# q's second half ahead of the weights, column 0 by feature tile, and a new list for the opening

## The chip, the cores and the metric

The program runs on one core of a Trainium2 chip. The metric is the device time in microseconds of one execution, taken as the median of several. The engines are TensorE (PE, with its weight loads as PEld), VectorE (DVE), ScalarE (ACT), GpSimd (POOL) and SyncE (SP), which here only issues DMAs.

## What is computed

Three layers, one after the other, in float32. Attention with 32 packed rows per head, twice (first the packed rows against k and v, then q against the packed rows), a gated layer, and a layer with a leaky ramp:

```python
def sm_attn(qq, kk, vv):            # scale, max, exp, sum, divide, times vv
    ...
p_packed = sm_attn(p, k, v)         # batch 8, heads 8, seq 576, head_dim 64, 32 packed rows
x = sm_attn(q, p_packed, p_packed)  # -> 4608 tokens x 512
gate = 1.0 / (1.0 + np.exp(-(x @ w_gate)))   # 512 x 1536
x = gate * (x @ w_val) @ w_out               # 1536 x 512
h = x @ w_in                                 # 512 x 2048
out = np.maximum(0.01 * h, h) @ w_out        # 2048 x 512
```

The weights arrive as 64-bit numbers and are read as pairs of 32-bit words.

## The kernel before

**Precision.** TensorE multiplies in a short float32 form, so an operand is split in a high part (a cast on ACT) and a low part (a subtraction, mostly on DVE), and three products stand for one: low by high, high by low, high by high.

**Weights.** A weight tile is loaded as 1024 word pairs per partition (L363). `unit` turns it into float32 in five passes: ACT scales the upper words (L307), ACT converts the lower words (L316), ACT puts in the sign (L324), DVE shifts (L332), POOL adds (L338). `unit_gv(i, g)` does this for column block i (256 features, two feature tiles of 128) of the gate weights (g = 0) or the value weights (g = 1); 6 column blocks, `wc[i]`. Column 0 alone is loaded and converted in two parts, by rows of the weights.

**Attention.** `attention(b)` loads k (L485), p (L479), q in two halves (L494) and v (L503, L507) of batch b; transposes k (L525, L529), p (L510) and q (L521) on DVE; scores of the packed rows (L540), their maximum (L568), exp (L576), sums and reciprocals (L587, L588), scaling (L594), flips through TensorE (L602) and copies (L612, L613), product with v (L622), packing (L634 to L650). Then q's scores (L540 again) in two halves of the tokens: `front` transposes them in PSUM (L655), takes the maximum (L663), subtracts it (L665) and takes exp (L674); `back` sums (L681, L682, L686), scales (L687), transposes (L695) and splits the weights of attention into `Ah` (L708, ACT) and `Al` (L710, DVE).

**Gated layer.** `gated(b)` multiplies the packed rows with column block i first (`m_mm`, L815, 16 matmuls), splits the result (`m_split`: cast to `mh`, L829, subtraction to `ml`, L832), and multiplies it with `Ah` and `Al` for each of 12 feature tiles f: 12 matmuls for the gate, 12 for the value (L848). ACT takes tanh (L857), DVE combines (L863), SP stores the tile to `g1d` in DRAM (L870).

**Other weights.** Beside the gated layers of all batches `staged` prepares 22 tiles of the three other weight matrices on ACT, DVE and POOL and stores them to DRAM (wp, wu and wd in the rows).

**Blocks.** Then five blocks of tokens (480 or 384 twice) go through the last three products, with 4620 matmuls (L1030), in Strassen's scheme of 7 products. Their weights come back from DRAM through SP (`load_weights`, L942, 512 KB each, tile name wu), their inputs from `g1d` through POOL's DMA queue (L1110), and are split by ACT (L971) and DVE (L976).

**Order.** No engine chooses by itself at run time: each does its instructions in the order in which they were written. `Plan` writes that order. Each task has an engine, a duration, a rank (lower goes first), tasks that it follows, and places in pools that it takes and gives. The plan runs through its own time; on each engine the ready task of lowest rank is written next. Urgent tasks that are soon ready keep others from starting. Between plan times 2 and 100 an idle PE gets filler matmuls (`keep`, L1271). The staged tiles have ranks from 200 in steps of 22; `open_left`, after which the first weight loads of the blocks may be written, follows when all staged tiles have begun their stores.

Of the kernel before, what the change touches and what calls it, by code (L numbers as in the profile page):

```python
# [10 lines left out]
F32 = mybir.dt.float32  # L11
# [8 lines left out]
P = 128  # L20
# [11 lines left out]
class Plan:  # L32
# [9 lines left out]
    def __init__(self):  # L42
        self.tasks, self.pools, self.holders, self.table = [], {}, {}, None
        self.begun, self.slots, self.where, self.lag = {}, {}, {}, {}
        self.urgent, self.keep = set(), None
# [5 lines left out]
    def add(self, engine, us, rank, fn, after=(), take=(), give=(), table=None, slack=None, begun=(), lag=3.5, urgent=False):  # L51
        i = len(self.tasks)
        if urgent:
            self.urgent.add(i)
        self.lag[i] = lag if engine == "DMA" else 0
# [10 lines left out]
    def run(self):  # L66
# [16 lines left out]
        soon = {e: {} for e in ready}  # L83
        while len(order) < n:
            for e, heap in ready.items():
# [3 lines left out]
                while heap:  # L89
# [7 lines left out]
                    if all(  # L97
# [82 lines left out]
def pack_attention_glu_lrelu(  # L180
# [100 lines left out]

    def unit(key, rank, dma_rank, loads, target, apart, home="raw64", after=()):

# [13 lines left out]
        def rows4(x, h):  # L297
            k = x.shape[1] // m
            return x[:, k * h:k * h + k]

        def scale(h):
            def fn():
                if "x" not in t:
# [3 lines left out]
                nc.scalar.activation(  # L307
                    x, word.rearrange("p (a b) -> p a b", a=x.shape[1]), AF.Copy, scale=2.0 ** -112
                )
# [34 lines left out]
        for h in range(len(loads)):  # L344
            L.append(add("DMA", 3.4 / len(loads), dma_rank + 0.1 * h, do_load(h),
# [3 lines left out]
        for h in range(m):  # L349
            need = [L[h]] if apart else L[-1:]  # L350
            a = add("ACT", us[0], rank + 0.1 * h, scale(h), [*need, *after, *made[-1:]])
            c = add("ACT", us[1], rank + 0.1 * h, low(h), [a], take=[("cv", ("cv", key))] if h == 0 else ())
            made.append(add("ACT", us[2], rank + 0.1 * h, sign(h), [c], give=[("raw", key)]))
            s = add("DVE", 0.75 if m == 1 else 0.5, (-91.5 if rank < -90 else -40 if rank < -44 else rank) + 0.1 * h, shift(h), [a])
            ends.append(add("POOL", 2.4 if m == 1 else 1.34, rank + 0.1 * h, total(h), [made[h], s], give=[("cv", key)]))
        return ends

    def unit_gv(i, g):
        w = (w_gate, w_val)[g]

        def load(j0, j1):
# [7 lines left out]
        first = i < 1  # L369
        rank = (-100 if i == 0 else -64 + 16 * i) + 2 * g  # L370
        return unit(
            ("gv", i, g), rank, (-71.05, -70)[g] if i == 0 else -60 + 4 * i + 2 * g, [load(0, 2), load(2, 4)] if first else [load(0, 4)],
            lambda: wc[i][:, :, g], first, HOMES[2 * i + g],
# [5 lines left out]
    def staged(st, g, kk, rank):  # L379
# [54 lines left out]
        a1 = add("POOL", 2.2, rank, combine(  # L434
            (2, 7, 1, ALU.add), (slice(3, 5), slice(2, 7, 4), slice(6, 8), ALU.subtract)
        ), whole)
        a2 = add("POOL", 0.82, rank, combine((5, 0, 3, ALU.subtract)), [a1])
        stored[key] = []
        for a, x0, x1 in ((a1, 0, 4), (a2, 4, 7)):
            n = (x1 - x0) * 256  # L440
            h = add("ACT", act(n), rank - 2000, high(x0, x1), [a], take=[("HL", (key, x0))])
            l = add("POOL", 0.7 + n * 0.0024, rank - 2000, low(x0, x1), [h], give=[y])
# [21 lines left out]
    def attention(b):  # L464
# [234 lines left out]
        def fin(half, part):  # L699
            def fn():  # L700
# [8 lines left out]
                else:  # L709
                    nc.vector.tensor_tensor(  # L710
# [5 lines left out]
        r1 = r0 - (60 if b else 80)  # L716
# [3 lines left out]
        tp = late("DVE", 0.43, r1, p_t, [Lp] + (packed[b - 1, "ck"] if b else []), give=[K("praw")[1]])  # L720
        tk = [
            late("DVE", 0.81 if b < 2 else 0.9, r1 + 0.1 * j, tr("k", j), [Lk[j // 2]], take=[K("w576", "tk", j)],
# [7 lines left out]
        mx = [late("DVE", 0.88 if b < 2 else 0.95, r1 + 2 + G, max1(G), [ck]) for G in range(2)]  # L730
        packed[b, "ck"] = [ck]
        ex = [
            late("ACT", 0.88 if b < 2 else 0.98, r1 + G, exp1(G), [mx[G]], take=[K("w576", "a", G)], give=[K("ps", "sk", G)[1]])
# [4 lines left out]
        r0 -= 20 * (b == 1)  # L738
        fl, un, norms = [], [], []
        for G in range(2):  # L740
# [3 lines left out]
            fl.append(late("PE", 0.8 if b < 2 else 1.25, r0 - 30 + G, flip(G), [nm], take=[K("ps", "f", G)],  # L744
# [559 lines left out]
```

## Time and profile before

| | us |
|---|---|
| three runs | 1426.91, 1429.21, 1429.30 |
| median | 1429.21 |
| profiled execution, its own time | 1425.92 |
| its span in the profile | 1424.1 |
| PE busy | 1408.0 (99%) |
| DVE, ACT, POOL busy | 977.5, 723.3, 474.8 |
| share of the chain that ended last: L1030, L848 | 67%, 22% |

Times in the rows are counted from the start of the span. PE's busy time holds the fillers too, so the opening looks fuller than it is: useful work is PE's time less the time of L1271. The execution has three stages: the opening, to about 71 us, in which batches 0 and 1 start and the fillers run; the gated layers with attention beside them, to 457.43; the blocks, to the end.

### The profile page before, as it was taken

The numbers are of one execution on the slowest core, as the hardware profiler recorded it, in microseconds if no ns is written. First come the engines' busy times: TensorE is split into PE (matmuls) and PEld (weight loads), VectorE is DVE, ScalarE is ACT, GpSimd is POOL, SyncE is SP. The second block draws the span as 40 slices with busy tenths as digits, with TensorE's granted clock in tenths as the row PEclk, the third lists the DMA queues.
The fourth block names the chain that finished last, engine by engine and source line by source line (L and its number), as shares of the span: only waits on it lengthen the run. The fifth ranks groups of instructions, "written<-read, shape, count | busy, mean of one in ns | idle before, by whom it ended". The sixth has DMA issues, their size and how long they took to land.

```text
span 1424.1 us, 24514 instructions
## 1 busy us (share of the span) xinstructions
PE 1408.0 (99%) x9724; PEld 1226.5 (86%) x9724; DVE 977.5 (69%) x1162; ACT 723.3 (51%) x855; POOL 474.8 (33%) x513
## 2 busy tenths in 40 slices
PE   8999999999999999999999999999999999999998
PEld 5788888888888888888888888888888888899997
DVE  6878778778755764778464987546984648785483
ACT  5876766776864434453244634345532446333460
POOL 1426873787885000056000156000460000460002
PEclk9999999999999999999999999999999999999999
DMA  9999998999878876698777798676997766998887
GB/s 316 271 279 312 324 309 272 330 319 336 307 267 322 278 231 205 202 339 256 209 227 203 246 312 242 207 232 198 307 288 208 222 205 210 319 275 253 255 253 184
DMA packets 146354, 374.93 MB, mean 263 GB/s; under 512 B 34544, under 2 KB 45136, under 8 KB 146240
## 3 DMA queue, kind: packets, MB, share of 16 engines
q1 hardware_dynamic: 115248, 295.76, 66.6%
q0 software_dynamic: 25696, 76.96, 15.5%
q8 instruction: 77, 1.26, 0.4%
q10 hardware_dynamic: 5296, 0.64, 0.3%
q14 instruction: 37, 0.30, 0.1%
HBM read 295.17 MB, written 78.12 MB: 262 GB/s over the span
## 4 chain that ended last, share of the span: by engine, by line
PE 95%; DVE 3%; DMA 1%; SPq 0%; issue 0%; ACT 0%; DVEq 0%
PE ps_pair L1030 67%; PE ps_pair L848 22%; PE ps_pair L815 3%; PE ps_pair L540 2%; DMA raw<-in_q_dram 1%; PE ps_pair L622 1%; DVE Al L710 0%; DVE ml L832 0%; DVE wc L332 0%; DMA raw<-in_k_dram 0%; PE ps_pair L1271 0%; PE ps_pair L602 0%; DVE sg L863 0%; DVE mx L663 0%; DVE ps_pair L655 0%; PE ps_pair L643 0%
## 5 line engine op out<-in xcount | busy, mean ns | idle before, releaser
L1030 PE MATMUL ps_pair<-op,wu 128*128 128x480 f32 (+1 forms) x4620 | 959.9, 370 | 0.0
L1030 PEld LDWEIGHTS ps_pair<-op,wu 128*128 128x128 f32 x4620 | 853.4, 188 | 106.3
L971 ACT CAST op<-rg 128x960 fp32r<-128x960 f32 (+1 forms) x280 | 259.6, 963 | 236.6 <-DVE rg L962 133.4
L976 DVE TENSOR_TENSOR op<-rg,op 128x960 fp32r<-128x960 f32 (+1 forms) x280 | 304.1, 1109 | 50.3 <-ACT op L971 49.5
L1110 POOL DMA_DIRECT2D rg<-g1d x96 | 68.7, 718 | 572.0 <-DVE op L976 170.4
L1047 DVE TENSOR_TENSOR tmp<-ps_pair,tmp 128x960 f32<-128x960 f32 (+1 forms) x60 | 67.0, 1117 | 194.3 <-PE ps_pair L1030 140.3
L962 DVE TENSOR_TENSOR rg<-rg 128x960 f32<-128x960 f32 (+1 forms) x160 | 177.4, 1111 | 6.0 <-DMA rg<-g1d 4.7
L848 PE MATMUL ps_pair<-Ah,ml 128*128 128x288 f32 x768 | 172.3, 305 | 0.5 <-DVE ml L832 0.4
L848 PE MATMUL ps_pair<-Al,mh 128*128 128x288 f32 x768 | 164.7, 295 | 0.7 <-DVE Al L710 0.7
L848 PE MATMUL ps_pair<-Ah,mh 128*128 128x288 f32 x768 | 164.8, 295 | 0.0
L848 PEld LDWEIGHTS ps_pair<-Ah,ml 128*128 128x128 f32 x768 | 122.1, 188 | 39.3 <-issue 14.3
L1217 POOL DMA_DIRECT2D out_dram<-os x208 | 124.2, 605 | 76.1 <-DVE os L1197 69.5
L848 PEld LDWEIGHTS ps_pair<-Al,mh 128*128 128x128 f32 x768 | 123.5, 188 | 0.9 <-DVE Al L710 0.9
L848 PEld LDWEIGHTS ps_pair<-Ah,mh 128*128 128x128 f32 x768 | 123.6, 188 | 0.0
L1041 ACT COPY tmp<-ps_pair 128x960 f32<-128x960 f32 (+1 forms) x60 | 55.7, 928 | 119.4 <-PE ps_pair L1030 119.4
L1162 ACT ACTIVATE rg<-rg 128x960 f32<-128x960 f32 (+1 forms) x80 | 78.0, 975 | 73.0 <-DVE rg L1158 71.6
L863 DVE SCALAR_TENSOR_TENSOR sg<-sg,ps_pair 128x576 f32<-128x576 f32 x96 | 71.8, 749 | 57.2 <-PE ps_pair L848 29.1
L417 POOL TENSOR_TENSOR HL<-Y,HL 128x1024 fp32r<-128x1024 f32 (+1 forms) x44 | 95.1, 2172 | 21.5 <-ACT HL L411 21.1
L857 ACT ACTIVATE sg<-ps_pair 128x576 f32<-128x576 f32 x96 | 62.4, 650 | 58.9 <-PE ps_pair L848 56.1
L338 POOL TENSOR_TENSOR Y<-Y,cvf 128x1024 int32<-128x1024 int32 x22 | 52.7, 2396 | 75.7 <-DVE Y L332 32.4
L832 DVE TENSOR_TENSOR ml<-ps_pair,mh 128x1024 fp32r<-128x1024 f32 x48 | 58.2, 1213 | 14.7 <-ACT mh L829 14.6
L829 ACT CAST mh<-ps_pair 128x1024 fp32r<-128x1024 f32 x48 | 48.6, 1012 | 35.9 <-PE ps_pair L815 35.8
(83 smaller groups left out, 938.6 us busy)
## 6 DMA issues: line engine op xcount, KB each, us to landing
wu<-wu SPq DMA_DIRECT2D x140, 512.0 KB, 3.9
wu<-wd SPq DMA_DIRECT2D x140, 512.0 KB, 4.3
wu<-wp SPq DMA_DIRECT2D x105, 512.0 KB, 4.5
g1d<-sg SPq DMA_DIRECT2D x96, 288.0 KB, 4.6
raw<-in_moe_w_out_dram SPq DMA_DIRECT2D x28, 512.0 KB, 6.7
raw<-in_k_dram SPq DMA_DIRECT2D x16, 576.0 KB, 6.4
rg<-g1d POOLq DMA_DIRECT2D x24, 384.0 KB, 6.2
rg<-g1d POOLq DMA_DIRECT2D x18, 480.0 KB, 7.8
```

The lines of the kernel that those rows point to most:

```text
L417: nc.gpsimd.tensor_tensor(out=hl[:, :, 1], in0=t["y"][:, x0:x1], in1=hl[:, :, 0].bitcast(F32), op=ALU.subtract,)
L848: nc.tensor.matmul(ps[:, t, :HS], w, x[:, t * HS:(t + 1) * HS], start=(n == 0), stop=(n == len(pairs) - 1),)
L857: nc.scalar.activation(st["sg", f], st["gv", f, 0][:, :, :HS], AF.Tanh, scale=0.5)
L863: nc.vector.scalar_tensor_tensor(out=sg, in0=sg, scalar=1.0, in1=st["gv", f, 1][:, :, :HS], op0=ALU.add, op1=ALU.mult)
L962: nc.vector.tensor_tensor(out=src(g, o), in0=src(g, a), in1=src(g, b), op=ALU.subtract)
L971: nc.scalar.copy(h, src(g, c))
L976: (nc.gpsimd if on_pool(i, g) else nc.vector).tensor_tensor(out=l, in0=src(g, c), in1=tiles["op", st, i, g][0].bitcast(F32), op=ALU.subtract)
L1030: nc.tensor.matmul(ps[c][:, m, :TB], a, x[:, kk, :], start=(fresh and kk == 0 and y == 0), stop=(end and kk == 1 and y == 2), skip_group_c ...
L1047: nc.vector.tensor_tensor(out=T[x], in0=ps[c][:, :, :TB], in1=T[y], op=ALU.add)
L1110: nc.gpsimd.dma_start(out=t[:, :, t0 - base:t0 - base + m], in_=g1d[b][:, f:f + 2, s0:s0 + m])
L1162: nc.scalar.activation(t, t, AF.Prelu, alpha=0.01, scale=0.5)
L1217: queues[turn % len(queues)].dma_start(out=ob[:, s0:s0 + m, d0:d0 + 32], in_=tiles["os", c][32 * y:32 * y + 32, x, t0:t0 + m],)
```

## The change

Four things are changed; line numbers move by 13 to 43 (L494 becomes L521, L332 L343, L363 L377 or, for column 0, L392, L655 L682, L710 L737, L815 L844, L829 and L832 L865 and L867, L848 L885, L870 L907, L942 L985, L1030 L1073).

1. The second half of q of batch 0 is loaded ahead of all weights. Column 0 is loaded by `unit_first(f)`, one feature tile of 128 features at a time, gate then value. The four loads are as large as before (512 KB) and have pieces of 1 KB in DRAM, not 2 KB.
2. Column 0's packed product and its split for batch 0 go by feature tile: 8 matmuls of 256 columns, a cast and a subtraction of 512, twice.
3. The ranks and durations of the opening's tasks are listed anew, for batches 0 and 1; the third load of column weights stands ahead of batch 1's k, and batch 1's q later. The plan counts that DVE and POOL can't do certain passes at once (`lock`).
4. The staged tiles have ranks from 256.35 in steps of 19.83.

On DVE three of column 0's four shifts stood ahead of the first L655 and the fourth ahead of the second; now two L343 stand ahead of both L682, which stand together, and two behind. The split of the first feature tile (L867) now stands ahead of the first half of `Al` (L737), and batch 1's k transposes (L552), two of which stood ahead of the second half of `Al`, stand behind it.

The options `GS` and `on_pool`, new in the code, are never on.

```diff
+                        if i in self.lock:
+                            begin, end = (now + x for x in self.lock[i])
+                            late = max(0.0, held["POOL" if e == "DVE" else "DVE"] - begin)
+                            us, held[e] = us + late, end + late
...
+    def unit_first(f):
+        def load(g):
+            def fn(raw):
+                nc.sync.dma_start(
+                    out=raw.rearrange("p (g j c) b -> p g j (c b)", g=2, j=NJ)[:, g],
+                    in_=(w_gate, w_val)[g][:, f * 256:(f + 1) * 256].rearrange("(j p) c -> p j c", p=P),
+                )
+            return fn
+
+        return unit(
+            ("gv", 0, f), -100 + 2 * f, (-70.9, -70)[f], [load(0), load(1)],
+            lambda: wc[0].rearrange("p j g (f c) -> p f g j c", f=2)[:, f], True, HOMES[f],
+        )
...
-        ld = (-100, -52.9)[b] if b < 2 else r1
+        ld = (-100, -50.75)[b] if b < 2 else r1
...
-        r0 -= 20 * (b == 1)
+        r0 -= -4.77 * (b == 1)
...
-        Lq = [add("DMA", 2.2 if b < 2 else 2.0, ((-72, -49)[b] if b < 2 else r1 + 3) + G, load_qk(q, "q", G), take=[K("qk", "q", G)], lag=LAG)
+        Lq = [add("DMA", 2.2 if b < 2 else 2.0, ((-72, -37.39)[b] if b < 2 else r1 + 3) + G, load_qk(q, "q", G), take=[K("qk", "q", G)], lag=LAG)
...
+            first = (b, i) == (0, 0)
+            low = {}
+            for f in range(2) if first else (None,):
+                r = -95 + 0.4 * (f or 0) if first else r0 + 16 * i - 60
...
-        rank = 200
+        rank = 256.35
...
-                    rank += 22
+                    rank += 19.83
```

Three places of the new order. First SP's queue at the very start, before:

```order
L494 DMA raw<-in_q_dram 128x576
L494 DMA raw<-in_q_dram 64x576 x2
L503 DMA v<-in_v_dram 64x8x256 x2
L507 DMA v<-in_v_dram 64x8x64
L363 DMA raw_250<-in_moe_w_gate_dram 128x2x512
L494 DMA raw<-in_q_dram 128x576
L494 DMA raw<-in_q_dram 64x576 x2
L363 DMA raw_250<-in_moe_w_gate_dram 128x2x512
L363 DMA raw_333<-in_moe_w_val_dram 128x2x512 x2
```

and after:

```order
L521 DMA raw<-in_q_dram 128x576
L521 DMA raw<-in_q_dram 64x576 x2
L530 DMA v<-in_v_dram 64x8x256 x2
L534 DMA v<-in_v_dram 64x8x64
L521 DMA raw<-in_q_dram 128x576
L521 DMA raw<-in_q_dram 64x576 x2
L392 DMA raw_300<-in_moe_w_gate_dram 128x4x256
L392 DMA raw_300<-in_moe_w_val_dram 128x4x256
L392 DMA raw_338<-in_moe_w_gate_dram 128x4x256
L392 DMA raw_338<-in_moe_w_val_dram 128x4x256
```

The second half of q has moved ahead of the first weight load; the second weight load still follows q and one other weight load.

Second, ACT around batch 1's exp, before (cvf is the lower words of a weight tile, w_804 and w_811 the two halves of batch 1's packed attention):

```order
L576 ACTIVATE w_804,sm<-ps_pair,mx 128x2x9x32
L576 ACTIVATE w_811,sm<-ps_pair,mx 128x2x9x32
L857 ACTIVATE sg<-ps_pair 128x576
L594 ACTIVATE w_804<-w_804,sm 128x576
L594 ACTIVATE w_811<-w_811,sm 128x576
L829 CAST mh<-ps_pair 128x1024
```

and after:

```order
L603 ACTIVATE w_825,sm<-ps_pair,mx 128x2x9x32
L603 ACTIVATE w_839,sm<-ps_pair,mx 128x2x9x32
L865 CAST mh<-ps_pair 128x1024
L335 ACTIVATE cvf<-Y 128x1024
L621 ACTIVATE w_825<-w_825,sm 128x576
L621 ACTIVATE w_839<-w_839,sm 128x576
```

Between the two exps and the two scalings stood one tanh; now a cast and a sign pass stand there.

Third, SP's queue at the end of the gated layers, before (g1d_64 is batch 7's tiles, wp_65 to wp_67 the first weights of the blocks):

```order
L870 DMA g1d_64<-sg 128x576 x8
L942 DMA wu<-wp_65 128x1024
L870 DMA g1d_64<-sg 128x576
L942 DMA wu<-wp_66 128x1024
L870 DMA g1d_64<-sg 128x576
```

and after:

```order
L907 DMA g1d_64<-sg 128x576 x11
L985 DMA wu<-wp_65 128x1024
L985 DMA wu<-wp_66 128x1024
L907 DMA g1d_64<-sg 128x576
L985 DMA wu<-wp_67 128x1024
```

The first weight load of the blocks stood behind 8 of batch 7's 12 stores and stands behind 11.

## Rows read from the trace of the kernel before

**Rows 1.** Windows: stretch, length, then busy time of PE, PEld, DVE, ACT, POOL, PEclk, DMA share, GB/s.

```profile
0.00:42.80 42.80, 35.78 (x453) 26.58 (x453) 29.40 (x62) 26.59 (x38) 8.21 (x11) 0.96 1.02 301
42.80:70.80 28.00, 26.36 (x394) 19.56 (x394) 24.49 (x46) 24.68 (x32) 12.21 (x5) 1.00 0.89 285
70.80:457.40 386.60, 386.08 (x4263) 327.23 (x4264) 282.91 (x448) 265.04 (x346) 261.76 (x191) 1.00 0.90 305
```

**Rows 2.** Windows of the fillers alone (L1271): stretch, length, busy time of PE, PEld.

```profile
0.00:42.80 42.80, 24.64 (x190) 19.02 (x190) 0.96 1.02 301
42.80:70.80 28.00, 4.09 (x29) 2.55 (x28) 1.00 0.89 285
```

**Rows 3.** Chain of waits: start, length, engine, tile, line.

```profile
23.76 1.48 DVE wc L332
...
34.40 1.23 DVE ml L832
...
39.55 0.59 DVE w L525
...
40.98 0.65 DVE Al L710
...
42.85 1.54 PE ps_pair L540 x55
...
444.45 12.98 PE ps_pair L848 x96
```

**Rows 4.** Timeline at 20 us: start, length, engine, line, operation, then idle before and its releaser.

```profile
20.14 0.78 DVE L521 STREAM_TRANSPOSE w<-raw 128x576 f32<-128x576 f32 x1 [6.38 <-DMA raw<-in_q_dram]
...
21.15 0.67 ACT L307 ACTIVATE wc<-raw 128x512 f32<-128x512 f32 x1 [0.91 <-DMA raw<-in_moe_w_gate_dram]
```

**Rows 5.** Timeline from 32 to 39 us: towards the first products of the gated layer.

```profile
32.67 0.75 DVE L710 TENSOR_TENSOR Al<-w,Ah 128x576 fp32r<-128x576 f32 x1
...
33.70 0.65 DVE L332 TENSOR_SCALAR wc<-wc 128x1024 int32<-128x1024 int32 x1
...
35.72 2.40 POOL L338 TENSOR_TENSOR wc<-wc,cvf 128x1024 int32<-128x1024 int32 x1 [6.42 <-ACT cvf L324]
...
36.43 0.38 PE L848 MATMUL ps_pair<-Ah,ml 128*128 128x288 f32 x1
...
36.83 1.90 DVE L687 TENSOR_TENSOR w<-w,sm 128x576 f32<-128x576 f32 x1
```

**Rows 6.** Windows while v comes in, and while column weights come in.

```profile
9.60:13.50 3.90, 3.59 (x47) 2.64 (x29) 3.39 (x10) 2.57 (x6) 0.00 (x0) 1.00 1.13 216
...
19.00:26.00 7.00, 4.52 (x79) 2.54 (x80) 5.69 (x12) 6.00 (x10) 3.17 (x3) 0.76 1.05 381
```

**Rows 7.** Timeline from 49 to 55 us: batch 1's scaling, its flips, ACT's neighbours.

```profile
49.78 0.77 ACT L594 ACTIVATE w<-w,sm 128x576 f32<-128x576 f32 x1 [1.42 <-DVE sm L588]
50.46 0.99 ACT L829 CAST mh<-ps_pair 128x1024 fp32r<-128x1024 f32 x1
...
50.61 0.77 PE L602 MATMUL ps_pair<-ident,w 128*128 128x128 f32 x5 [0.25 <-ACT w L594]
...
53.83 1.37 ACT L324 ACTIVATE cvf<-Y 128x1024 f16<-128x1024 f32 x1
```

**Rows 8.** Timeline of SP's queue: the weight load behind the eleventh store of batch 7.

```profile
456.22 0.43 SPq L942 DMA_DIRECT2D wu<-wp  x1
```

**Rows 9.** DMA issues at 456 to 457 and 444.9 to 457: KB each, median us to landing.

```profile
wu<-wp SPq DMA_DIRECT2D x1, 512.0 KB, 5.9
...
wu<-wp SPq DMA_DIRECT2D x5, 512.0 KB, 7.4
```

**Rows 10.** The page's DMA issues of the whole span, the same loads.

```profile
wu<-wp SPq DMA_DIRECT2D x105, 512.0 KB, 4.5
```

**Rows 11.** Windows around PE's idle time in the opening: the idle stretch, then what follows.

```profile
18.96:21.46 2.50, 0.00 (x0) 0.00 (x0) 1.29 (x4) 1.56 (x3) 0.08 (x1) 1.00 1.06 379
...
22.16:25.57 3.41, 3.41 (x68) 1.62 (x53) 3.35 (x6) 3.35 (x7) 1.95 (x3) 0.50 1.05 384
```

More of the change, by code (lines that the diff above doesn't have):

```diff
@@ L49, in pool, with add @@
         self.slots[name] = list(range(n))
-    def add(self, engine, us, rank, fn, after=(), take=(), give=(), table=None, slack=None, begun=(), lag=3.5, urgent=False):
+    def add(self, engine, us, rank, fn, after=(), take=(), give=(), table=None, slack=None, begun=(), lag=3.5, urgent=False, lock=None):
         i = len(self.tasks)
@@ L83, in run @@
         soon = {e: {} for e in ready}
+        held = {"DVE": 0.0, "POOL": 0.0}
         while len(order) < n:
@@ L344, in unit @@
         for h in range(len(loads)):
-            L.append(add("DMA", 3.4 / len(loads), dma_rank + 0.1 * h, do_load(h),
+            L.append(add("DMA", 3.4 / len(loads) - (0.1 if rank < -90 else 0), dma_rank + 0.1 * h, do_load(h),
                          take=[(home, ("raw", key))] if h == 0 else (), begun=L[:1], lag=LAG))
@@ L441, in staged @@
             h = add("ACT", act(n), rank - 2000, high(x0, x1), [a], take=[("HL", (key, x0))])
-            l = add("POOL", 0.7 + n * 0.0024, rank - 2000, low(x0, x1), [h], give=[y])
+            l = add("POOL", 0.7 + n * 0.0024, rank - 2000, low(x0, x1), [h], give=[y], lock=(0, n * 0.0024))
             stored[key].append(add("DMA", n / 340, rank, store(x0, x1), [l], give=[(key, x0)], lag=6))
@@ L729, in attention @@
         )
-        mx = [late("DVE", 0.88 if b < 2 else 0.95, r1 + 2 + G, max1(G), [ck]) for G in range(2)]
+        mx = [late("DVE", 0.88, r1 + 2 + G, max1(G), [ck]) for G in range(2)]
         packed[b, "ck"] = [ck]
         ex = [
-            late("ACT", 0.88 if b < 2 else 0.98, r1 + G, exp1(G), [mx[G]], take=[K("w576", "a", G)], give=[K("ps", "sk", G)[1]])
+            late("ACT", 0.88, r1 + G, exp1(G), [mx[G]], take=[K("w576", "a", G)], give=[K("ps", "sk", G)[1]])
             for G in range(2)
@@ L754, in attention @@
         p2 = late("PE", 0.45, r0 - 27, pack2, [p1])
-        p3 = late("DVE", 0.3, r0 - 27 if b else -90.8, pack3, [p2], take=[K("pps")], give=[K("ps", "pp")[1]])
+        p3 = late("DVE", 0.3, r0 - 27 if b else -92, pack3, [p2], take=[K("pps")], give=[K("ps", "pp")[1]])
         packed[b] = p3
@@ L762, in attention @@
         sb = []
-        c = late("PE", 1.5, r0 + (-28 if b < 2 else 9), scores2, [p1, *tq], take=[K("ps", "sq", h) for h in range(2)],
+        c = late("PE", 1.5, r0 + (-26.5 if b < 2 else 9), scores2, [p1, *tq], take=[K("ps", "sq", h) for h in range(2)],
                  give=[K("w576", "tq", j)[1] for j in range(NJ)])
@@ L779, in back @@
             a = late("ACT", act(576), r if b else -200, fin(h, 0), [a, begin])
[L780 removed]
+            on_pool = b == 0 and h < 0
+            fins.append(late("POOL" if on_pool else "DVE", 1.6 if on_pool else 0.75, r, fin(h, 1), [a], lock=(0, 1.6 if on_pool else 0.73),
                             give=[K("w576", "u", h)[1]]))
@@ L882, in gated @@
                     g, vv = [
-                        add("PE", 0.8, r - 0.5 + 0.1 * g, mm(f, g, range(1)), [l, ready_a[b][0]], take=[K("ps", f, g)], urgent=True)
+                        add("PE", 0.8, r - 0.5 + 0.1 * g, mm(f, g, range(1)), [low[f % 2 if first else 0], ready_a[b][0]], take=[K("ps", f, g)], urgent=True)
                         for g in range(2)
```

117 lines of the change are left out of this document (67 added, 50 removed).

## The prediction, made before the change was run

> **What bounds the kernel now.** I read the windows by stage first, then the fillers in the same windows, then the chain of waits, then the timeline at the places where the chain leaves PE. The windows show three stages [rows 1]. From 70.8 to 457.4 PE is busy 386.08 of 386.60 us, and the chain runs through PE's matmuls there and in the blocks: what starts earlier at 70.8 ends earlier by as much, and only a hole in PE's row costs anything. Before 70.8 PE's time is mostly fillers, to be taken out [rows 1, 2]: useful work leaves 42.80 - 35.78 + 24.64 = 31.7 us of the first 42.8 us empty, and 28.00 - 26.36 + 4.09 = 5.7 us of the next 28.0. So the opening is where time can be won. There the chain runs over DVE: a shift of column 0's weights at 23.76 (1.48 us, where it needs 0.4), the split `ml` at 34.40, k transposes from 39.55, the second `Al` at 40.98 [rows 3]. The second place to look at is the seam at 457.43 (444.45 + 12.98, [rows 3]), where PE goes from L848 to L1030 with no gap; whatever is late there is a hole of PE.
>
> **Loads of the opening.** Before, q's third transpose waits for its load until 20.14, and the second scaling of column 0 for its own until 21.15 [rows 4]. q's second half goes ahead of one 512 KB load, which at 381 GB/s [rows 6] takes 1.4 us, so the third transpose should start at about 18.5. That alone gives little: the second weight load stands where it stood, behind q and one other weight load, and its scaling stays at about 21.5 to 22. Its shift is in DVE's row ahead of the first L682, behind POOL's first addition, and ends at 23.6. What is gone is the third shift with its wait, so the first L682 starts at about 23.7 and not at 23.76 + 1.48 = 25.24 [rows 3]: 1.5 us.
>
> Pieces of 1 KB in DRAM appear in no weight load of the trace; v's pieces are of 1 KB, and while v comes in the rate is 216 GB/s against 381 for the weights of 2 KB pieces [rows 6]. Bounds: at 381 GB/s a weight load takes 1.4 us and the change costs nothing; at 216 it takes 2.4, two loads are 2.1 us later, 0.3 of it is slack in front of the second shift, and the opening is 1.8 us longer. Below nothing there is no case, as the bytes are the same. I take nothing: the weight rows are the nearer ones, with the same bytes, queue and 128 partitions, where v's loads go to 64 each. The Trainium skill (SBUF — State Buffer, Door 1: The DMA port swizzle) says that a load's rate follows from how many of 16 ports its partitions reach, and that 64 partitions in a row reach 8 of them. By that rule v is slow for its partitions and not for its pieces, and the term is nothing; if pieces of 1 KB were the cause, it is the 1.8 us. The row for v agrees in size but tells the two causes not apart.
>
> **First products.** Before, the first L848 starts at 36.43, after `ml` (34.40 + 1.23 = 35.63, whole) although `Al` was done at 32.67 + 0.75 = 33.42 [rows 3, 5]. Now half a split stands ahead of `Al`, so `Al` ends last: 33.42, less 1.5 for the start above, plus 0.8 because the second L682 no longer fills the wait for the first exp but stands ahead of the maximum (one transpose, 0.79 as L521 takes 0.78, [rows 4]), plus 0.65 for the half split (half of 1.23 and a little), plus 0.6 because L714 meets POOL's fourth addition (before, L687 took 1.90 us while L338 ran from 35.72 for 2.40 us, [rows 5]). That is 34.0, a gain of 2.4.
>
> The second half of `Al` starts the rest. Before, it ends at 40.98 + 0.65 = 41.63 [rows 3], 8.2 us behind the first. Of these 8.2 go: a shift, 0.65 [rows 5]; two k transposes, 40.98 - 39.55 = 1.4 [rows 3]; the block of L687, which by the first half's equal transposes of 0.77 should take about 0.75 and took 1.90, 1.15 [rows 5]; half of the split, 0.6; and 0.5 comes back, since ACT's cast `Ah` is no longer hidden by the k transposes. The second half follows the first by 4.9 and stands at 38.9 to 39.0: **gain 2.6**. As the lost time of this stretch is made up only of such waits, all of it is a shift of the rest.
>
> **Batch 1's flips.** From 39.0, 36 products at 12.98 / 96 = 0.135 us [rows 3] take 4.9, to 43.9; batch 1's scores take 1.5 [rows 3], from 44.2 to 45.7; column 1's packed product ends at 46.7. The next work is batch 1's flips. Before, they started at 50.61, 7.8 after the scores began at 42.8 [rows 1, 7]. Now a cast (0.99) and a sign pass (1.37, [rows 7]) stand between exp and scaling, together 2.4; a tanh (0.65 by its place between the two) leaves it, and the 1.42 us in which L594 waited for DVE [rows 7] are covered: 44.2 + 7.8 + 2.4 - 0.65 - 1.4 = 52.4. PE has only fillers from 46.7 to 52.4, less 0.3 around it: 5.4. Behind it I count 0.85 and 0.9 us ahead of the packed products of columns 2 and 3, which wait for POOL's additions, and 0.25 in small gaps: 7.4 lost against 5.7 [rows 1, 2]: **loss 1.6 to 1.7**. Bounds: if ACT's order costs nothing, 5 of the 7.4 go and the term is a gain of 3; if POOL's additions drag as well, a loss of 3. I take 1.6. The additional 8 short matmuls of the packed product cost 0.1 at most. On SP's queue a third column load now stands ahead of batch 1's k, and its q behind more weights: 1.4 us each [rows 6]. k is wanted only at 40, by DVE's order, and q only by scores behind the products of columns 1 and 2, so I cost both at nothing; that cover gone, they would cost those 1.4.
>
> So the opening gives -2.6 + 1.6 + 0.1 = -0.9, between -3.5 and +2.
>
> **The seam.** This is the part that the words of the change leave out. The last staged tile has rank 256.35 + 21 x 19.83 = 673, not 200 + 21 x 22 = 662; a batch has 100 ranks and takes about 50 us, so the staged work ends some 6 us later, and the plan writes the first weight load of the blocks behind 11 of batch 7's stores, not 8. SP waits at each store for its tile; behind it is queued every load. Before, a weight load stands right behind the eleventh store and was issued at 456.22 [rows 8], 1.2 us ahead of the seam. That one took 5.9 us to land [rows 9], at 462.1: as first load it would have held PE from 457.43 for 4.65 us. So the price is read from the very place: **4.6 us**. Bounds: the median of all such loads, 4.5 us [rows 10], gives 3.3; the five loads of this stretch, 7.4 [rows 9], give 6.2. Nothing hides it: all L848 of batch 7 are done, no product of the blocks has its weights, and the inputs that POOL's queue brings don't depend on this order. The loads behind it come each 1.2 to 1.5 us while a group of 12 products takes 2.5, so there is one hole and not many.
>
> **The clock.** In the opening PE was idle for 2.50 us and the granted clock in the 3.41 us of work after it was 0.50 [rows 11], the lower level; 3.41 x 0.5 = 1.7 us of work lost. The hole at the seam is longer and holds no fillers. Bounds 0 and 1.7; I take the middle, 0.9, since that idle stretch followed only fillers, this one follows dense work.
>
> **The sum.** -0.9 + 4.6 + 0.9 = +4.6. The profiled execution's own time is 1425.92 (1.8 us of it outside the span, which I leave as they are), so a like one of the changed kernel is at 1430.5. The median of the three runs is 3.29 above the profiled execution; I add the sum to the median: **1433.8**.
>
> **Rivals.** First, *no change that can be told* (0.2% of this kernel, 2.9 us, is about what a measurement can tell; the band is 1426.35 to 1432.07). The first load lands in 4.5 us as most do, and the clock stays up: +3.3 - 0.9 = +2.4, 1431.6. It decides at a landing of 5 us. For it: 105 loads have that median [rows 10]; against it: the last transfers of batch 7 and POOL's loads are on the queues at just that time, and the stretch's own loads are the slow ones [rows 9].
>
> Second, *slow weights*: 1 KB pieces go at v's rate, +1.8 on the forecast, 1435.6. For it: the only row of such pieces [rows 6]; against it: that row's partitions differ.
>
> Third, the other side, *faster*: ACT's cast and sign pass are done by the time DVE has batch 1's reciprocals, so the empty 5.4 us before the flips shrink to 1 and one of the two later holes closes: -0.9 - 4.4 - 0.9 = -6.2 for the opening, and with the seam at 3.3 that is -2.9, 1426.3. It decides where the flips start before 48 us. For it: before, L594 waited for DVE and not for ACT [rows 7]; against it: 2.4 us of ACT passes stand in a row that was full, and the gain has to outrun the seam.
>
> Fourth, that the change doesn't do what it says: q's second half early is of no use, since DVE then waits for column 0's second load [rows 4]. I hold this as likely, and it is in the sum: q's share of the gain is small, the third shift's is the 1.5.
>
> **Chances.** Forecast 0.56, slow weights 0.12, no change 0.25, faster 0.07. So slower by over 0.2% 0.68, within 0.2% 0.25, faster 0.07. The range leaves out the faster case and the tails: low 1429.3 (the seam at 3.3, the clock kept and the opening near its lower bound, -3.2), high 1436.8 (the seam at 6.2, the clock at 1.7, the opening at -0.3).
>
> **What would show it.** In the profile after: the third q transpose (L548) at 18.5; first L682 at 23.7; first L885 at 34.0, its second half at 39; fillers alone from 46.7 to 52.4 ahead of L629; the first weight load of the blocks (L985) issued 1 to 2 us ahead of the last L885's end, and PE idle for 4.6 us before the first L1073, with a clock of 0.5 behind it. I am wrong if PE goes from L885 to L1073 without a hole, or if the lost time before 70.8 falls by more than 4 us.

## The result, and the profile after

The changed kernel took 1435.46 us (median of 4; 1434.62 to 1436.63), the kernel before 1428.38 us in the same comparison (1426.91 to 1429.30). The ratio is 1.0055, with an interval of 1.0043 to 1.0068: it is slower by 7.1 us, where 4.6 were forecast. The time lies in the stated range.

From the page of the changed kernel, the busy times and the row of the blocks' products:

```profile
span 1433.2 us, 24570 instructions
PE 1409.9 (98%) x9740; PEld 1228.5 (86%) x9740; DVE 979.9 (68%) x1163; ACT 723.9 (51%) x856; POOL 474.1 (33%) x513
...
L1073 PE MATMUL ps_pair<-op,wu 128*128 128x480 f32 (+1 forms) x4620 | 963.3, 370 | 7.4 <-DMA wu<-wp 7.4
```

The first line to look at is the last one: the blocks' products were 7.4 us idle for their weights. Before, they began without a gap behind L848, whose last products end at 444.45 + 12.98 = 457.43 [rows 3]; the chain of waits before has them as one piece (start, length, what):

```profile
457.43 959.77 PE ps_pair L1030 x4620
```

In the changed kernel a store and a transfer stand in the chain at this place:

```profile
456.36 0.76 DVE sg L900
457.12 0.02 issue
457.13 0.32 SPq L907
457.45 0.05 issue
457.50 12.36 DMA wu<-wp
469.87 0.14 issue
470.00 956.07 PE ps_pair L1073 x4596
```

PE's timeline at the seam shows two waits, and SP's queue what they wait for:

```profile
455.02 0.42 PE L885 MATMUL ps_pair<-Ah,mh 128*128 128x288 f32 x2
462.56 7.20 PE L1073 MATMUL ps_pair<-op,wu 128*128 128x480 f32 x24 [7.12 <-DMA wu<-wp]
470.00 15.23 PE L1073 MATMUL ps_pair<-op,wu 128*128 128x480 f32 x69 [0.24 <-DMA wu<-wp]
```

```profile
454.74 0.80 SPq L985 DMA_DIRECT2D wu<-wp  x2
457.13 0.32 SPq L907 DMA_DIRECT2D g1d<-sg  x1
457.50 12.61 SPq L985 DMA_DIRECT2D wu<-wp  x6
```

PE leaves L885 at 455.4, 2.0 us earlier than before (457.4). The first two weight loads are issued at 454.7 and 455.1, and the first takes 7.7 us to land. The third stands behind the twelfth store, which waits for DVE's last tile; it is issued at 457.5 and takes 12.4 us. Product 25 of the blocks starts at 470.00, 14.6 us behind the end of L885; before it started 5.0 behind it (462.47). So the seam costs 9.5 us. The two spans differ by 9.1: -2.0 in front of the seam, +9.5 at it, +1.4 spread over the blocks, +0.2 in the tail. (The profiled execution of before, 1425.92, was a quick one of its kind, so 9.1 of the spans stand against 7.1 of the medians.)

The granted clock at the seam, by windows of PE's hole and of what follows (stretch, length, busy time of PE, PEld, DVE, ACT, POOL, PEclk, DMA share, GB/s):

```profile
455.44:462.56 7.12, 0.00 (x1) 0.03 (x1) 7.12 (x8) 3.99 (x5) 4.94 (x7) 0.79 1.03 395
462.56:466.06 3.50, 3.50 (x9) 2.94 (x10) 3.46 (x4) 0.00 (x0) 0.00 (x0) 0.50 1.04 410
```

The granted clock is at its lower level (0.50) for the 3.5 us behind the hole, as it was behind the idle stretch of [rows 11].

The opening, from the timeline of all engines:

```profile
18.24 1.44 DVE L548 STREAM_TRANSPOSE w<-raw 128x576 f32<-128x576 f32 x2 [3.96 <-DMA raw<-in_q_dram]
...
19.39 0.66 ACT L320 ACTIVATE wc<-raw 128x512 f32<-128x512 f32 x1 [3.33 <-DMA raw<-in_moe_w_gate_dram]
...
22.06 1.07 DVE L343 TENSOR_SCALAR wc<-wc 128x512 int32<-128x512 int32 x1 [0.55 <-ACT wc L320]
23.05 1.45 DVE L682 STREAM_TRANSPOSE ps_pair<-ps_pair 128x576 f32<-128x576 f32 x2
```

The first product follows at 32.64 (before 36.43, [rows 5]), the second half's first at 38.14, batch 1's flips at 50.97. To see how much of this gain lasts I take PE's timeline and subtract, at a time t, what the useful matmuls started until then take at their usual spacing. What is left is lost time, in us:

| t | 43 | 60 | 72 | 240 | 440 |
|---|---|---|---|---|---|
| before | 33.1 | 36.3 | 40.1 | 46.6 | 52.1 |
| changed | 29.5 | 35.8 | 37.4 | 43.3 | 50.1 |

The opening wins 3.6 us, has given 3.1 back at 60, wins again where the kernel before lost 2.6 us at 64.6, and keeps 2.0 at the end.

### The profile page after: what moved, and what is told of

The parts are those of the page before. It is cut to its first block, busy times and chain, and to the rows that moved or that the text cites. A ratio compares the mean times of both kernels' runs of the same rounds, so it can differ in the third digit from the quotient of the medians.

```text
span 1433.2 us, 24570 instructions
## 1 busy us (share of the span) xinstructions
PE 1409.9 (98%) x9740; PEld 1228.5 (86%) x9740; DVE 979.9 (68%) x1163; ACT 723.9 (51%) x856; POOL 474.1 (33%) x513
## 4 chain that ended last, share of the span: by engine, by line
PE 81%; DMA 1%; DVE 0%; issue 0%; SPq 0%; DVEq 0%
PE ps_pair L1073 67%; PE ps_pair L885 12%; PE ps_pair L844 2%; DMA wu<-wp 1%; PE ps_pair L567 1%; PE ps_pair L649 0%; PE ps_pair L629 0%; PE ps_pair L670 0%; DVE rg L1240 0%; DVE ml L867 0%; DVE tmp L1231 0%; DVE sg L900 0%; SPq L907 0%; DVE op L1019 0%; DVEq L900 0%
## 5 line engine op out<-in xcount | busy, mean ns | idle before, releaser
L1073 PE MATMUL ps_pair<-op,wu 128*128 128x480 f32 (+1 forms) x4620 | 963.3, 370 | 7.4 <-DMA wu<-wp 7.4
L1073 PEld LDWEIGHTS ps_pair<-op,wu 128*128 128x128 f32 x4620 | 855.2, 188 | 115.4 <-issue 7.9
L885 PE MATMUL ps_pair<-Ah,ml 128*128 128x288 f32 x768 | 171.8, 304 | 2.2 <-DVE ml L867 1.9
L885 PE MATMUL ps_pair<-Al,mh 128*128 128x288 f32 x768 | 164.7, 295 | 0.2 <-DVE Al L737 0.2
L885 PE MATMUL ps_pair<-Ah,mh 128*128 128x288 f32 x768 | 164.9, 295 | 0.0
L885 PEld LDWEIGHTS ps_pair<-Ah,ml 128*128 128x128 f32 x768 | 122.3, 188 | 36.6 <-DVE sg L900 10.9
L885 PEld LDWEIGHTS ps_pair<-Al,mh 128*128 128x128 f32 x768 | 123.6, 188 | 0.4 <-DVE Al L737 0.4
L885 PEld LDWEIGHTS ps_pair<-Ah,mh 128*128 128x128 f32 x768 | 123.6, 188 | 0.0
L867 DVE TENSOR_TENSOR ml<-ps_pair,mh 128x1024 fp32r<-128x1024 f32 (+1 forms) x49 | 58.5, 1196 | 17.7 <-ACT mh L865 17.5
L432 POOL TENSOR_TENSOR Y<-Y 128x256 f32<-128x256 f32 (+1 forms) x66 | 63.3, 960 | 4.1
```

The costliest lines, as they stand in the source:

```text
L432: nc.gpsimd.tensor_tensor(out=y[:, o], in0=y[:, a], in1=y[:, b], op=op)
L885: nc.tensor.matmul(ps[:, t, :HS], w, x[:, t * HS:(t + 1) * HS], start=(n == 0), stop=(n == len(pairs) - 1),)
L1073: nc.tensor.matmul(ps[c][:, m, :TB], a, x[:, kk, :], start=(fresh and kk == 0 and y == 0), stop=(end and kk == 1 and y == 2), skip_group_c ...
```

## The experiments

**Which of the parts makes the hole.** First the staged ranks by themselves: back to the old ones in the changed kernel, and the new ones alone in the kernel before.

```diff
-        rank = 256.35
+        rank = 200
...
-                    rank += 19.83
+                    rank += 22
```

> The changed kernel with the staged tiles' ranks as before (from 200 in steps of 22); the opening stays changed. In its order the first weight load of the blocks stands behind 8 of batch 7's stores again. My theory (the staged ranks alone make the hole of 7 us at the seam and the wait for the third load): no hole over 0.5 us between L885 and L1073, and the opening's 2.0 us (PE leaves L885 at 455.4 and not 457.4) are kept: about 1426.4, 0.15% faster than before, 9 us faster than the change. Rival (the hole comes from the opening: PE is at the seam 2 us earlier and the loads are not): hole of 2 us or more, 1428.4 or slower.

Measured: 1425.34 us, ratio to the kernel before 0.9985 (0.9976 to 0.9994). PE's timeline has no hole:

```profile
454.47 15.77 PE L1073 MATMUL ps_pair<-op,wu 128*128 128x480 f32 x72
```

> The kernel before with the staged tiles' ranks alone changed (from 256.35 in steps of 19.83). In its order all twelve stores of batch 7 stand ahead of the first weight load. My theory: the load is issued at about 458.3, behind the last store, and lands 6 to 12 us later; hole of 7 to 12 us, 1436 to 1441. Rival (ranks alone do nothing, the relisted opening is what costs): 1428.4, within 1.5.

Measured (the same edit the other way round, in the kernel before): 1438.03 us, ratio 1.0079 (1.0066 to 1.0091), with one wait of 8.75 us:

```profile
465.64 14.54 PE L1030 MATMUL ps_pair<-op,wu 128*128 128x480 f32 x53 [8.75 <-DMA wu<-wp]
```

In this run all twelve stores stand ahead of the first load. The loss is larger than the wait, since the granted clock behind it is at its lower level, and here no later wait covers that:

```profile
465.60:470.00 4.40, 4.36 (x11) 3.70 (x12) 4.06 (x4) 0.00 (x0) 0.00 (x0) 0.50 1.03 395
```

The first 24 products take 8.1 us, where they took 5.2 before.

So the two numbers of the staged ranks are the whole loss, and the opening by itself is a gain of 2 us. What in these ranks does it is not settled by that.

**SP's order against late work.** The prediction put the hole down to SP's order. Two runs take order and lateness apart. One has the late staged work with SP's old order, the other the early staged work with the new order.

```diff
...
+        for x, y in ((8, 1), (9, 2), (10, 4), (11, 5)):
+            plan.begun[g1_done[B - 1][x]] = first_loads[:y]
```

> The changed kernel, staged ranks as in the change, but SP's order at the seam as before: batch 7's stores 9 to 12 stand behind the first 1, 2, 4 and 5 weight loads. All other staged work is as late as in the change. My theory (SP's order, in which loads are queued behind stores that wait for tiles): loads issued from 446 to 449, the first lands by 456, hole under 1 us, 1426 to 1428. Rival (the staged work ends too late, and the loads wait for their room in memory whatever SP's order is): first load issued after 452, hole of 4 us or more, 1432 to 1436.

Measured: 1434.06 us (1.0046; 1.0033 to 1.0059), only 1.4 us less than the change, and the two intervals overlap. The first load was issued at 447.9. With the old ranks it was issued at 442.2; here SP waited 5.0 us until the last staged store had landed (in us: total, times, longest):

```profile
SPq L987 <- DMA wd<-HL: 5.0, 1, 5.0
```

And the loads landed late. The five loads issued from 447 to 457, KB each and median us to landing, and PE's timeline:

```profile
wu<-wp SPq DMA_DIRECT2D x5, 512.0 KB, 12.7
```

```profile
459.45 2.84 PE L1078 MATMUL ps_pair<-op,wu 128*128 128x480 f32 x12 [1.36 <-DMA wu<-wp]
463.74 5.44 PE L1078 MATMUL ps_pair<-op,wu 128*128 128x480 f32 x24 [1.45 <-DMA wu<-wp]
471.33 4.01 PE L1078 MATMUL ps_pair<-op,wu 128*128 128x480 f32 x12 [2.15 <-DMA wu<-wp]
```

My theory falls here. The rival holds in part: the first load did wait for its room, 5.0 us, and the time is in the rival's range. But it was issued at 447.9 and not after 452, and the wait for room is not all: from issue to landing the five loads then took a median of 12.7 us.

```diff
...
+        plan.begun[first_loads[0]] = [g1_done[B - 1][10]]
+        plan.begun[first_loads[1]] = [g1_done[B - 1][10]]
+        plan.begun[first_loads[2]] = [g1_done[B - 1][11]]
```

> The changed kernel with the staged ranks of before (from 200 in steps of 22), and SP's order at the seam as in the change: the first two weight loads behind eleven of batch 7's stores. The opposite of the run with the order alone. It measures the term of the prediction by itself. Theory of the prediction (the order on SP makes the hole; the first load is issued about 1.2 us ahead of the seam and lands in 5 to 7): hole of 4 to 6 us, and with the third load behind the last store some 2 more: 1430 to 1432. Rival (the order does nothing, the late end of the staged work makes the whole hole): 1425.3, as with the staged ranks of before.

Measured: 1428.20 us, 1.0004 (0.9995 to 1.0013); that is 2.9 us above the run with the old staged ranks and the old order. The two loads behind eleven stores landed in 4.2 us and the hole is 2.24 us:

```profile
wu<-wp SPq DMA_DIRECT2D x2, 512.0 KB, 4.2
```

```profile
458.27 12.00 PE L1078 MATMUL ps_pair<-op,wu 128*128 128x480 f32 x54 [2.24 <-DMA wu<-wp]
```

All four cases, with the changed opening (the last column is the time from the end of L885 to product 121 of the blocks in the one profiled execution):

| staged work | SP's order | us | waits of PE at the seam | to product 121 |
|---|---|---|---|---|
| early | as before | 1425.34 | none | 25.9 |
| early | as in the change | 1428.20 | 2.24 | 29.0 |
| late | as before | 1434.06 | 1.36, 1.45, 2.15, 0.38 | 33.6 |
| late | as in the change | 1435.46 | 7.12, 0.24 | 35.5 |

By the medians the lateness costs 7 to 9 us and the order 1.4 to 2.9, where the 1.4 is not clear of the noise; by the last column 6.5 to 7.7 and 1.9 to 3.2. With late work the old order brings product 25 forward, from 14.6 us behind L885 to 8.4, but the loads behind it are late in their turn. About 1 us of the 33.6 is the lower clock: behind the wait of 2.15 products 55 to 60 come 0.40 us apart.

**What the lateness is.** POOL's timeline shows when the last staged stores and the blocks' first inputs were issued; before, changed, and with the old ranks:

```profile
432.48 1.53 POOL L425 DMA_DIRECT2D wd<-HL  x2
434.00 4.24 POOL L1110 DMA_DIRECT2D rg<-g1d  x6
```

```profile
438.09 1.54 POOL L452 DMA_DIRECT2D wd<-HL  x2
439.62 4.96 POOL L1153 DMA_DIRECT2D rg<-g1d  x7
```

```profile
427.74 1.53 POOL L452 DMA_DIRECT2D wd<-HL  x2
429.26 4.24 POOL L1153 DMA_DIRECT2D rg<-g1d  x6
```

The staged work ends 5.6 us later than before and 10.4 later than with the old ranks. Counted back from the end of L885, its stores are issued 15.8 us ahead in the change, 23.4 before and 25.4 with the old ranks. The windows of 435 to 445 and 445 to 457 say what that means to the DMA engines (the last two columns: share and GB/s); before, changed, old ranks:

```profile
435.00:445.00 10.00, 10.00 (x91) 8.00 (x90) 3.49 (x4) 2.71 (x4) 5.38 (x8) 1.00 1.01 316
445.00:457.00 12.00, 12.00 (x92) 12.00 (x91) 8.89 (x9) 5.50 (x8) 1.42 (x2) 1.00 1.03 407
```

```profile
435.00:445.00 10.00, 10.00 (x83) 9.00 (x83) 3.96 (x4) 3.97 (x5) 9.58 (x11) 1.00 0.65 218
445.00:457.00 12.00, 10.44 (x79) 10.21 (x77) 5.05 (x6) 4.51 (x6) 4.10 (x6) 1.00 1.01 351
```

```profile
435.00:445.00 10.00, 10.00 (x84) 8.99 (x83) 5.93 (x6) 4.89 (x7) 2.85 (x5) 1.00 1.01 380
445.00:457.00 12.00, 12.00 (x85) 11.70 (x84) 7.87 (x10) 5.23 (x7) 2.06 (x3) 1.00 0.97 370
```

Before, the engines are full from 435 on. In the change they are at 0.65 until 445: POOL computes the last staged tile until 438.1 and issues the inputs behind its stores, from 439.6 on, and the eighth input waits 3.44 us for a staged store to land, a wait for room:

```profile
448.02 0.70 POOL L1153 DMA_DIRECT2D rg<-g1d  x1 [3.44 <-DMA wd<-HL]
```

Against the kernel before, (316 - 218) x 10 + (407 - 351) x 12 = 1650 KB are not moved by 457, 4 us at 400 GB/s. They are moved afterwards, beside the weights, by engines that are full in both kernels (share 1.03 in front of 470). To test that, a run adds bytes and nothing else to the kernel without a hole:

```diff
...
+        for x in range(5):
+            nc.gpsimd.dma_start(
+                out=extra[:, x].rearrange("p a b c -> p (a b c)"),
+                in_=wsd["p", 0][:, x].rearrange("p a b c -> p (a b c)"),
+            )
```

> The changed kernel with the staged ranks of before, which has no hole at the seam, and five more transfers of 512 KB from DRAM to DRAM (2.6 MB, written to a place that nobody reads) on POOL's queue right ahead of the blocks' first inputs. No instruction of PE, DVE or ACT and no order on SP is changed: it puts in bytes alone. My theory now (late bytes on DMA engines that are full are what made the hole): 2.6 MB at 400 GB/s are 6.5 us of them; 3 to 4 us lie between the first weights' landing (450.6) and their use (454.5), so a hole of 2 to 5 us and 1427 to 1431. Rival (the hole came from the computing of the late staged tiles or from room in memory): within 0.7 of the kernel without them, 1425.3.

Measured: 1432.16 us (1.0040; 1.0027 to 1.0052), 6.8 us more in the medians than without them; the 2.6 MB at 400 GB/s are 6.5. I had reckoned with 3 to 4 us of slack, the time between the first weights' landing and their use, and it was of no use: the first who waited was not PE for weights but DVE, in whose row an operand of the blocks stands ahead of batch 7's last split. PE and DVE:

```profile
451.13 0.85 PE L885 MATMUL ps_pair<-Ah,ml 128*128 128x288 f32 x2 [4.64 <-DVE ml L867]
```

```profile
448.78 1.16 DVE L1026 TENSOR_TENSOR op<-rg,op 128x960 fp32r<-128x960 f32 x1 [7.43 <-DMA rg<-g1d]
449.85 1.22 DVE L867 TENSOR_TENSOR ml<-ps_pair,mh 128x1024 fp32r<-128x1024 f32 x1
```

So bytes alone, on DMA engines that are full, can make a loss of this size. How they make it in the change is not shown by this run: there PE waited for weights and not for DVE, the extra transfers stand in POOL's own queue ahead of the inputs, and 1650 KB are 4 us, not 7 to 9. How the rest divides between the wait for room and the transfers' queue stays open. Last of this group, how little it takes:

```diff
-                    rank += 19.83
+                    rank += 19.32
```

> The changed kernel with the staged tiles' start at 256.35 as in the change and a step of 19.32 in place of 19.83, so that the last rank is 662 as before; the plan lets the blocks' loads begin some 6 us earlier than in the change. My theory now (what counts is when the staged work ends, since its transfers and the inputs and weights of the blocks share DMA engines that are full at the seam): no hole over 1 us, 1425 to 1427, as with the ranks of before. Rival (the late start of the staged work, which leaves less of it to be done beside the first batches, costs by itself): 1429 or slower.

Measured: 1424.38 us, 0.9975 (0.9965 to 0.9985), no hole: 11 us less than the change for a step that is 2.6% smaller. The last staged stores are issued 22.9 us ahead of the end of L885, and the plan writes the first weight load behind eight stores again. The late start of the staged work costs nothing; its late end does, with the order on SP that follows from it.

**The clock.** The hole filled with 40 filler matmuls:

```diff
-            if self.keep and free["PE"] <= now and self.keep[0] <= now < self.keep[1] and self.pools["ps"][0] > 0:
+            if self.keep and free["PE"] <= now and (self.keep[0] <= now < self.keep[1] or 454 <= now < 460.5) and self.pools["ps"][0] > 0:
```

> The changed kernel with 40 filler matmuls in the hole between L885 and L1073. It separates the clock from the loads. In the change the first 24 products of the blocks took 7.4 us where 24 x 0.216 = 5.2 is full speed, at a granted clock of 0.50 for 3.5 us, and then PE waited for the third load at 469.87. My theory now (the third load ends last, so the clock's 2 us lie beside it): granted clock 1.0 in the first products, but a wait of about 2 us in front of product 25, time within 0.7 of the change. Rival (my prediction's term: the clock costs 0.9 to 1.7 on top): 1 to 2 us faster than the change.

Measured: 1432.77 us (1.0045; 1.0032 to 1.0058), an interval that overlaps that of the change. PE's timeline:

```profile
460.92 5.41 PE L1073 MATMUL ps_pair<-op,wu 128*128 128x480 f32 x24 [2.00 <-DMA wu<-wp]
468.39 11.80 PE L1073 MATMUL ps_pair<-op,wu 128*128 128x480 f32 x46 [2.06 <-DMA wu<-wp]
```

The 24 products now take 5.4 us and not 7.2, and then PE waits 2.06 for the third load. From the end of L885 (453.84 here) to product 25 it is 14.55 us, against 14.56 in the change. Up to there the lower clock cost nothing: its 2 us lay beside that wait. But the fillers did not keep the clock up for good. Behind the second wait it falls all the same, and products 30 to 38 come 0.40 us apart and not 0.22:

```profile
468.39:472.00 3.61, 3.61 (x11) 3.08 (x12) 0.00 (x0) 0.00 (x0) 0.00 (x0) 0.63 1.02 399
```

No wait covers it there, and product 121 starts 37.1 us behind L885, 1.6 later than in the change. The median is 2.7 us below that of the change, which is nearer to the rival's forecast than to mine; the profile has this gain in front of the seam and behind product 121, not at the seam. That L885 ended 1.6 us earlier than in the change, with the same order up to there, shows how far single executions differ.

**The opening.** Three runs take its parts: q first alone, tiles alone (the list's numbers and the staged ranks as before; two of the lines), and q first with the list but no tiles. The first:

```diff
-            ("gv", i, g), rank, (-71.05, -70)[g] if i == 0 else -60 + 4 * i + 2 * g, [load(0, 2), load(2, 4)] if first else [load(0, 4)],
+            ("gv", i, g), rank, (-70.5, -70)[g] if i == 0 else -60 + 4 * i + 2 * g, [load(0, 2), load(2, 4)] if first else [load(0, 4)],
```

> The kernel before with q's second half ahead of all weight loads, nothing else: the same ranks, column 0 by rows. By the prediction (DVE then waits for column 0's second load, so the early half is of little use): third q transpose at about 18.5, first L655 and first product where they were within 0.7, time within 0.8 of the kernel before. Rival (q's load is what holds the opening): first product 1 us or more earlier and 1 us or more faster.

Measured: 1432.08 us (1429.35 to 1433.23), 1.0033 (1.0021 to 1.0046). Third transpose at 18.17 and first product at 35.77 as expected, but the first L655 at 22.90, 2.3 us earlier, and the time is outside my bound. The profiled execution (1429.35) has PE's last L848 0.8 us later than before; it does not show the other 4 us of the median. Open.

Tiles alone:

```diff
-        r0 -= -4.77 * (b == 1)
+        r0 -= 20 * (b == 1)
...
-            r = r0 + 9 + h if b else -91 + -0.64 * h
+            r = r0 + 9 + h if b else -91 + 1.0 * h
```

> The staged ranks and the opening's ranks of before, q's second half behind the first weight load as before; only column 0's loads, packed product and split go by feature tile. My theory (q's early half and the list take the third shift and the k transposes off DVE's path; the tile split is worth only what stands between the split and the first product): first product 0.5 to 1.5 us earlier than before, second half of Al where it was within 0.7, time within 0.8 us of the kernel before. Rival (the tile split is what gains the 3 us in the opening): 1.5 to 3 us faster than the kernel before.

Measured: 1431.41 us, 1.0025 (1.0015 to 1.0035). First product at 34.39, 2.0 earlier, second half at 40.86; then the lost time is 38.1 at 60 us, 1.8 more than before, and more holes follow (2.0 at 83, 1.6 at 147). Both sides were wrong: the tiles alone are a loss.

Q first and the list, without tiles (the loads and the split go back to rows and the whole as well):

```diff
...
-            for f in range(2) if first else (None,):
+            for f in (None,):
```

> The changed opening with q first and the new list, and the staged ranks of before, but column 0 loaded, multiplied and split whole, by rows, as before. With the run of the tiles alone it tells what the 2 to 2.8 us of the opening come from. My theory (the third shift and the k transposes off DVE's path give most): Al's first half ends where it does in the change within 0.7, the first product follows the whole split 1 to 2 us later, second half within 0.7; 1425 to 1427. Rival (without the half split the list gains nothing): 1427.2 or slower.

Measured: 1425.24 us, 0.9988 (0.9980 to 0.9997), the same as with the tiles (1425.34). The first product is at 35.06, 2.2 later than with them, and PE's lost time at 440 us is 51.6 against 49.3 with the tiles; yet the medians agree. The list with q first makes the gain of 2 us; the list without q first was not run. In the two profiles the tiles' 2.3 us are lost again behind the seam: with the tiles the products from the 121st on take 1.1 us more and the tail behind the last product 1.4 more. Why is not explained, and both are within what single executions differ by.

The wait ahead of the flips, in the kernel with the old staged ranks:

```diff
...
+                nm = add("DVE", 0.3, -88 + G, norm1(G), [ex[G]], slack=0.2, urgent=True)
+                norms.append(nm)
+                nm = add("ACT", 0.78, -88 + G, scale1(G), [nm], slack=0.2, urgent=True)
```

> The kernel with the staged ranks of before and the changed opening, and in it batch 1's norms and scalings ahead of the sign pass on ACT. In the change PE had fillers alone for 5.0 us ahead of the flips at 50.97. My theory (ACT's order holds the flips): they start 1.0 to 1.4 us earlier, and most of it is kept: 0.5 to 1.4 us faster than with the staged ranks of before alone, 1424 to 1425. Rival (another wait, for POOL's addition ahead of the packed products of columns 2 and 3, takes what is gained): same within 0.4.

Measured: 1423.71 us, 0.9979 (0.9970 to 0.9988), which overlaps the run without the edit (0.9976 to 0.9994). The flips start at 50.1 and not 51.2. At 79 us PE has a new hole of 3.7 us, where DVE's L714 takes 1.95 us beside an addition of POOL:

```profile
78.14 2.39 POOL L349 TENSOR_TENSOR wc<-wc,cvf 128x1024 int32<-128x1024 int32 x1 [4.33 <-DVE wc L343]
...
79.21 1.95 DVE L714 TENSOR_TENSOR w<-w,sm 128x576 f32<-128x576 f32 x1
```

> The two best parts together: the changed kernel with a step of 19.32 and batch 1's scalings ahead of the sign pass. If both add up (2.8 and 0.9 us): 1423.5, 0.25% faster than before. Rival (the earlier flips are given back at the next wait for POOL's addition, as the scalings alone gave back 3.7 us at 79 us): 1424.4 as with the step alone, or slower.

Measured (both edits): 1427.15 us, 1.0000 (0.9991 to 1.0009), with the same hole, 3.65 us at 80. The gains don't add; the step alone, 1424.38, beats both kernels.

## Why the prediction was right, and where it was not

**Side and place** were right: slower, by the staged ranks, at the seam, by a wait for the first weight load (7.12 us), with a lower clock behind it. The sum of +4.6 came near +7.1 with parts that were each off, and that is partly luck: the seam with its clock was forecast at 5.5 and cost 9.5 in the spans, the opening was forecast at -0.9 and gave -2.0, and the two errors offset each other in part.

**Loads.** The early start came as worked out: third transpose at 18.24 (18.5), first L682 at 23.05 (23.7), the second shift as the last thing in front of it. Pieces of 1 KB cost next to nothing: the four scalings of column 0 started at 19.39, 21.35, 23.28 and 25.17, 1.9 us apart as ACT's own work, and only the first waited for its load; at v's rate the loads would be 2.4 apart. The rival of slow weights falls. The Trainium skill (SBUF — State Buffer, Door 1: The DMA port swizzle) lets a load's rate follow from the ports that its partitions reach; these starts, 1.9 us apart, agree with it, as the weight loads go to all 128 partitions.

**Opening.** Forecast -0.9, measured -2.0 at the end of L885 and -2.1 in the run with the old staged ranks (1425.34 against 1427.47). First product 1.4 us earlier than forecast, second half 0.9, flips 1.4. The wait before the flips was there at 5.0 (5.4). Mis-sized was the loss behind it, forecast as 7.4 from 42.8 to 70.8 against 5.7: by the table of lost time it is 7.9 from 43 to 72 in the change but 7.0 before, so the loss is 0.9 and not 1.6. Two steps of this part don't hold as worked out. The flips before started at 50.61 only for the second half; the first half's five ran from 49.65, so the forecast of 52.4 counts from a start that is 1.0 too late. And a lower bound of -3.5 for the opening does not follow from its terms, as -2.6 - 3 + 0.1 is -5.5; with it the low end of the range would be about 1427. The measured -2.0 lies within both.

**The seam.** Here the step failed that read the price: "That one took 5.9 us to land, ... as first load it would have held PE", and with it "the inputs that POOL's queue brings don't depend on this order", "one hole and not many": the loads behind the first were to come each 1.2 to 1.5 us, and the third landed 7 us behind it. I had the staged work 6 us late (it was 5.6) and used that for the order of SP's queue alone. The order by itself costs 1.4 to 2.9 us; with early staged work the loads behind eleven stores land in 4.2 and not 5.9. The lateness costs 7 to 9: the last staged tile holds the room of the blocks' inputs and weights, the DMA engines run at 0.65 until 445 where they were full before, and in the change the first load takes 7.7 us to land and the third 12.4. That the late bytes are the whole way from lateness to loss is argued and not shown; they account for 4 us. A window of the trace of before would have warned me: DMA share 1.01 and 1.03 from 435 on. I took a landing time from one schedule to another, where the same load took from 4.2 to 12.7 us by what else the engines had to move.

**The clock.** The lower level came as forecast, its price of 0.9 did not: up to product 25 it cost nothing, as the distances of the run with fillers show. A slower engine in front of a wait for something else costs only what goes beyond the wait; I added the two. Where no wait follows, as with the staged ranks alone, the first 24 products took 2.9 us more than before, over the upper bound of 1.7.

**Rivals.** No change needed a landing under 5 us: the first took 7.7, the third 12.4. Faster needed the flips before 48: they were at 51.0. That q's early half does little by itself is neither shown nor refuted: the first L655 came earlier with it alone, and the time was worse.

## What to carry to other kernels

Where two stages meet and the DMA engines are full, count the bytes that must have passed by then and when their issue becomes possible; a load's landing time in such a stretch depends on what else is on the engines and can't be taken over to another schedule. Look for the last task that holds memory of the old stage, since it lets the transfers of the new one begin: here a step of ranks that was 2.6% smaller was worth 11 us. Measure a hand-tuned order part by part: q first alone and tiles alone each lost 4 to 5 us, while the list with q first won 2.

## What the runs showed of the hardware

The same load of 512 KB took a median of 4.2 us to land where the DMA share was 0.63 in the window of 445 to 457 in which it was issued (early staged work, late order), and 12.7 us in the kernel with SP's old order and late staged work, where the share was 1.01 in that window. DMA engines at a share of 1.01 to 1.03 moved between 316 and 407 GB/s, so the share alone doesn't tell the rate.

Behind idle stretches of PE of 7.12 us (the change) and 8.75 us (staged ranks alone) the granted clock was 0.50, and the blocks' products came 0.40 us apart and not 0.22. In the run with fillers it was 1.00 over the first 24 products and 0.63 over the 3.61 us behind the next wait of 2.06 us.

From their 121st to their last, the blocks' products took 933.6 us in the profile of before, 934.8 in the change and 935.4 in the run without a hole, at a granted clock of 1.00 in each. Differences under 2 us between single profiles of this kernel are not to be explained by an edit.
